# Clamps ahead of sums on GpSimd, a fourth weight chunk finished later and ScalarE's bits a step early, in an FFT-mixing and feed-forward kernel

## The chip, the cores and the metric

The kernel runs on one core of one Trainium2 chip. The metric is the device time of one launch in microseconds (us). The core has a matrix engine (TensorE, PE in the profile), VectorE (DVE), ScalarE (ACT), GpSimd (POOL) and a queue engine that issues transfers (SP). Each has its own instruction stream, and engines wait for each other by semaphores.

## The reference

```python
# x (8, 3008, 256) f32, w_in (256, 2048) f32, w_out (2048, 256) f32
X = np.fft.fft(np.fft.fft(x, axis=1), axis=2).real.astype(np.float32)
t = X.reshape(8 * 3008, 256)
h = t @ w_in
g = h * (1.0 / (1.0 + np.exp(-1.702 * h)))
out = (g @ w_out).astype(np.float32)        # (24064, 256)
```

## The kernel before

Almost all of the time is a loop of 384 steps: TensorE makes two blocks of hidden values (`hidden`, tiles pa and pb), VectorE combines them (`rows`), ScalarE applies the activation (`activate`), and TensorE multiplies by the second weights three steps later (`product`, tile po). This is about the first 82 us, in which weights are prepared while the first transform runs.

Weights arrive in eight 1 MB chunks of 64-bit numbers (in0 to in3, out0 to out3) and are rounded to 32 bits on the chip. For one chunk:

```python
def squares(key, eng): ...        # L368, VectorE or ScalarE: g = hi * hi
def clamp(key, lo=0, n=1024):     # L371, GpSimd: m = min(max(hi, -TOP), TOP)
    nc.gpsimd.tensor_scalar(...)
def low_up(key): ...              # ScalarE: the low bits, first half
def low_down(key): ...            # L381, ScalarE: the low bits, second half -> r
def bounds(key):
    prepare(key); squares(key, nc.scalar); clamp(key); low_up(key); low_down(key)
def high(key, lo=0, n=1024):      # VectorE, needs g and m; a is a single buffer
    dve.scalar_tensor_tensor(m, g, LOW * LOW, m, ...)    # L398
    dve.tensor_scalar(a, bits, ...)                      # L399
    dve.scalar_tensor_tensor(a, bits, 0xC0000000, a, ...)# L400
def finish_in(n, ...):            # L412, GpSimd: wst = a + r, an integer sum
def finish_out(n): ...            # L420, GpSimd: wo = a + r, two sums
def round_chunk(key):
    bounds(key)
    high(key)
    (finish_out if key[0] == "out" else finish_in)(key[1])
# ... cut ...
def fold_w(n, between=()):        # TensorE: 2 x 2 passes of 512 columns, tile psw;
    ...                           # ScalarE copies psw into wcs after each two
def first_row(n):                 # TensorE: one-column products, tile psf -> af2
```

An in-chunk goes on to TensorE (`fold_w`), which multiplies it by a small cosine and sine matrix; only then can steps use it. Steps 0 to 3 of the loop use the folds of in0 and in1, steps 4 to 7 those of in2 and in3, and so on in turn. PSUM tiles of folds, first rows, stage two and hidden values share four banks in turn. The part ahead of the loop, and the loop's schedule:

```python
            for h0 in (0, 512):          # in0 in two halves
                clamp(in0, h0, 512)
                high(in0, h0, 512)
                finish_in(0, h0, 512)
    # ... loads issued, cut ...
    squares(in1, nc.vector); clamp(in1); low_up(in1); low_down(in1); high(in1); finish_in(1)
    fold_w(0)
    prepare(out0); squares(out0, nc.vector); clamp(out0); low_up(out0); low_down(out0)
    high(out0); finish_out(0)
    warm(3)                              # matmuls whose result nobody reads
    rotate(0, 0, 4, nc.scalar.copy)
    stage2(0, 0)                         # second stage of the transform: PE, then VectorE transposes
    prepare(in2); squares(in2, nc.scalar); clamp(in2)
    fold_w(1, ((low_up, in2), (low_down, in2)))
    high(in2); finish_in(2)
    first_row(0)
    # ... cut ...
    for t, key in (2, ("out", 1)), (3, ("in", 3)), (5, ("out", 2)), (6, ("out", 3)):
        at(t, round_chunk, key)
    early[2], early[4] = 2, 3            # fold_w(2) in step 2, fold_w(3) in step 4
    rows_at = {1: 1, 3: 2, 5: 3}         # first_row
    for t in range(n + LAG):             # LAG = 3
        if t < n: hidden(t)
        if t == 0: nyquist(0, 0)         # the broadcast row that rows() needs
        if t in rows_at: first_row(rows_at[t])
        if t >= LAG: product(t - LAG)
        if t in early: fold_w(early[t])
        # activate(t-1), sums, rows(t), combine, then what at() put there
```

## Time and profile before

| | before |
|---|---|
| time, three runs | 1932.56 us (1932.33 to 1935.51) |
| the profiled execution | 1935.1 us, span 1933.3 us |
| PE busy in the first 82 us | 69.22 us |
| PE busy from 82 to 1900 us | 1818.00 us of 1818.00 |
| PE at half clock, up to its last matmul | 17.1 us, in three stretches |

One thing about this table matters for everything below: the execution that was profiled took 1935.1 us, so it is a slow one of its kind by 2.5 us.

In rows in order of time, the columns are: start in us, busy us, engine, line, operation, output<-input, shape, how many instructions were joined, and in brackets the idle time before them with what ended it.

### The profile page before, as it was taken

The numbers are of one execution on the slowest core, as the hardware profiler recorded it, in microseconds if no ns is written. First come the engines' busy times: TensorE is split into PE (matmuls) and PEld (weight loads), VectorE is DVE, ScalarE is ACT, GpSimd is POOL, SyncE is SP. The second block draws the span as 40 slices with busy tenths as digits, with TensorE's granted clock in tenths as the row PEclk, the third lists the DMA queues.
The fourth block names the chain that finished last, engine by engine and source line by source line (L and its number), as shares of the span: only waits on it lengthen the run. The fifth ranks groups of instructions, "written<-read, shape, count | busy, mean of one in ns | idle before, by whom it ended". The sixth has DMA issues, their size and how long they took to land.

```text
span 1933.3 us, 29337 instructions
## 1 busy us (share of the span) xinstructions
PE 1914.2 (99%) x10722; PEld 1677.6 (87%) x10722; DVE 1414.6 (73%) x2937; ACT 670.7 (35%) x923; POOL 764.0 (40%) x1057
## 2 busy tenths in 40 slices
PE   8899999999999999999999999999999999999998
PEld 5698888988889888898889888898888988889887
DVE  6577776877778677876777777777776777777776
ACT  4533333333333333333333333333333333333332
POOL 4275323543246332562235523265323642223222
PEclk9899999999999999999999999999999999999999
DMA  8620450227203362125322162221720223202201
GB/s 289 151 49 10 103 71 12 49 55 113 17 12 59 49 109 17 22 48 102 56 28 48 35 94 47 22 49 43 115 25 13 17 46 58 17 12 27 17 12 23
DMA packets 144912, 103.54 MB, mean 54 GB/s; under 512 B 104770, under 2 KB 127586, under 8 KB 143584
## 3 DMA queue, kind: packets, MB, share of 16 engines
q1 hardware_dynamic: 143424, 100.62, 31.1%
q8 instruction: 85, 1.39, 0.3%
q10 hardware_dynamic: 1344, 1.05, 0.2%
q14 instruction: 59, 0.48, 0.1%
HBM read 58.38 MB, written 48.01 MB: 55 GB/s over the span
## 4 chain that ended last, share of the span: by engine, by line
PE 96%; DVE 1%; DMA 1%; POOL 1%; issue 0%; ACT 0%; SPq 0%; POOLq 0%; DVEq 0%
PE po L542 59%; PE pa L475 17%; PE pb L475 17%; PE ps L213 1%; PE ps L320 1%; DMA raw<-in_moe_w_in_dram 1%; PE psw L439 1%; POOL wst L412 0%; DMA xt<-in_x_dram 0%; DVE m L398 0%; POOL m L371 0%; DVE a L400 0%; PE ps L217 0%; DVE a L399 0%; POOL wo L420 0%
## 5 line engine op out<-in xcount | busy, mean ns | idle before, releaser
L542 PE MATMUL po<-s,wo 128*128 128x256 f32 (+1 forms) x3008 | 758.7, 375 | 0.0
L516 POOL TENSOR_TENSOR s<-h 128x256 f32<-128x256 f32 (+1 forms) x376 | 270.6, 720 | 1086.2 <-ACT h L504 1021.6
L542 PE MATMUL po<-h,wo 128*128 128x256 f32 (+1 forms) x2384 | 689.7, 375 | 0.0
L542 PEld LDWEIGHTS po<-s,wo 128*128 128x128 f32 x3008 | 571.5, 190 | 64.5
L479 ACT COPY v<-pa 128x512 f32<-128x512 f32 (+1 forms) x384 | 222.0, 578 | 1062.4 <-PE pa L475 1062.4
L489 DVE TENSOR_TENSOR h<-v,pb 128x512 f32<-128x512 f32 (+1 forms) x384 | 258.8, 674 | 394.7 <-PE pb L475 390.8
L542 PEld LDWEIGHTS po<-h,wo 128*128 128x128 f32 x2384 | 452.8, 190 | 51.6
L504 ACT ACTIVATE h<-h 128x1024 f32<-128x1024 f32 (+1 forms) x384 | 400.8, 1044 | 17.9 <-DVE h L499 16.3
L475 PE MATMUL pa<-pq,wcs 128*128 128x256 f32 (+1 forms) x1536 | 394.2, 379 | 0.2 <-ACT af L452 0.2
L475 PE MATMUL pb<-pq,wcs 128*128 128x256 f32 (+1 forms) x1536 | 388.4, 375 | 0.0
L492 DVE SCALAR_TENSOR_TENSOR dif<-nb,af,pb 128x256 f32<-128x256 f32 (+1 forms) x768 | 328.1, 468 | 0.0
L475 PEld LDWEIGHTS pa<-pq,wcs 128*128 128x128 f32 x1536 | 286.8, 190 | 47.5 <-issue 10.8
L475 PEld LDWEIGHTS pb<-pq,wcs 128*128 128x128 f32 x1536 | 292.4, 190 | 33.4
L517 POOL TENSOR_TENSOR s<-h 128x256 f32<-128x256 f32 (+1 forms) x376 | 276.5, 735 | 0.0
L499 DVE TENSOR_TENSOR h<-pa,dif 128x512 f32<-128x512 f32 (+1 forms) x448 | 265.4, 604 | 13.2
L520 DVE TENSOR_TENSOR s<-h,s 128x256 f32<-128x256 f32 (+1 forms) x376 | 198.9, 529 | 12.9
L519 DVE TENSOR_TENSOR s<-s,h 128x256 f32<-128x256 f32 (+1 forms) x376 | 180.4, 480 | 4.3 <-POOL s L516 4.3
L199 POOL TENSOR_TENSOR xt<-xt 111x510 f32<-111x510 f32 x56 | 73.4, 1311 | 4.4
L576 DVE TENSOR_TENSOR c<-u,po 128x256 f32<-128x256 f32 (+1 forms) x188 | 69.3, 409 | 1.6
L326 DVE STREAM_TRANSPOSE pq<-ps 128x256 f32<-128x256 f32 x96 | 34.6, 417 | 43.9 <-PE ps L320 43.9
L576 DVE TENSOR_TENSOR u<-u,po 128x256 f32<-128x256 f32 (+1 forms) x141 | 57.6, 409 | 9.5 <-ACT u L547 4.6
L559 DVE STREAM_TRANSPOSE os<-c 128x512 f32<-128x512 f32 x94 | 61.0, 686 | 0.1
(72 smaller groups left out, 509.9 us busy)
## 6 DMA issues: line engine op xcount, KB each, us to landing
out_dram<-os SPq DMA_DIRECT2D x284, 64.0 KB
Td<-xt SPq DMA_DIRECT2D x14, 768.0 KB
t<-Td SPq DMA_DIRECT2D x7, 1536.0 KB
xt<-in_x_dram SPq DMA_DIRECT2D x14, 512.0 KB
xt<-Xr SPq DMA_DIRECT2D x14, 512.0 KB
nb<-pq SPq DMA_DIRECT2D x23, 256.0 KB
out_dram<-os SPq DMA_DIRECT2D x96, 56.0 KB
Xr<-in_x_dram SPq DMA_DIRECT2D x7, 752.0 KB
```

The costliest lines, as they stand in the source:

```text
L475: nc.tensor.matmul(ps[:, i * 256:i * 256 + n], lhsT=wcs[cs][:, f * 128:(f + 1) * 128], rhs=pq[:, cs, ks], start=True, stop=True)
L479: nc.scalar.copy(two(v[:], n), two(pa[:], n))
L489: nc.vector.tensor_tensor(two(h[:], n), two(v[:], n), two(pb[:], n), op=ALU.add)
L492: nc.vector.scalar_tensor_tensor(dif[:, i * 256:i * 256 + n], nb[:, ks], af2[:, f:f + 1], pb[:, i * 256:i * 256 + n], op0=ALU.mult, op1=AL ...
L499: nc.vector.tensor_tensor(free(h[:], 512 + at + m - 1, [256, 2], [RUN, blocks], [-1, m]), *ins, op=ALU.add)
L504: nc.scalar.activation(g, g, ACTF.Gelu_apprx_sigmoid)
L516: eng.tensor_tensor(s1, a21, a22, op=ALU.add)
L517: eng.tensor_tensor(s3, a11, a21, op=ALU.subtract)
L519: eng.tensor_tensor(s2, s1, a11, op=ALU.subtract)
L520: eng.tensor_tensor(s4, a12, s2, op=ALU.subtract)
L542: nc.tensor.matmul(pot[q][:, i, :n], lhsT=lhs, rhs=rhs, start=(p == 0 and i == 0 and f == 0), stop=(p == NP - 1), skip_group_check=True)
L576: nc.vector.tensor_tensor(out_, i0, i1, op=how)
```

## The change

The intent is to take three waits out of the first 82 us. On GpSimd, the clamp of the next chunk goes ahead of the sum of the last, so that VectorE always has a clamped chunk to work on. The high part and sum of in2, the third in-chunk to be folded (fourth to be rounded, after in0, in1 and out0), go into the loop behind VectorE's rows of steps 0 and 1, and the folds of in2 and in3 come one step later. For chunks in the loop, ScalarE's work and the clamp (`bounds`) come one step before VectorE's high part, and the sum one step after.

```diff
-    def round_chunk(key):
-        bounds(key)
-        high(key)
+    def finish(key):
         (finish_out if key[0] == "out" else finish_in)(key[1])
 # ... one memset placed later, warm(7) is warm(6): cut ...
             for h0 in (0, 512):
                 clamp(in0, h0, 512)
+            for h0 in (0, 512):
                 high(in0, h0, 512)
-                finish_in(0, h0, 512)
 # ... loads: cut ...
     prepare(in1)
+    clamp(in1)
     squares(in1, nc.vector)
-    clamp(in1)
+    for h0 in (0, 512):
+        finish_in(0, h0, 512)
     low_up(in1)
     low_down(in1)
     high(in1)
-    finish_in(1)
+    warm(4)
     fold_w(0)
     prepare(out0)
+    clamp(out0)
+    finish_in(1)
     squares(out0, nc.vector)
-    clamp(out0)
+    warm(1)
+    rotate(0, 0, 4, nc.scalar.copy)
+    stage2(0, 0)
     low_up(out0)
     low_down(out0)
-    high(out0)
-    finish_out(0)
-    warm(3)
-    rotate(0, 0, 4, nc.scalar.copy)
-    stage2(0, 0)
     prepare(in2)
     squares(in2, nc.scalar)
     clamp(in2)
     fold_w(1, ((low_up, in2), (low_down, in2)))
-    high(in2)
-    finish_in(2)
+    high(out0)
+    finish_out(0)
     first_row(0)
 # ... cut ...
-    for t, key in (2, ("out", 1)), (3, ("in", 3)), (5, ("out", 2)), (6, ("out", 3)):
-        at(t, round_chunk, key)
-    early[2], early[4] = 2, 3
-    rows_at = {1: 1, 3: 2, 5: 3}
+    for t, key in (1, in2), (2, ("out", 1)), (3, ("in", 3)), (5, ("out", 2)), (6, ("out", 3)):
+        at(t, high, key)
+        if key != in2:
+            at(t - 1, bounds, key)
+        at(t + 1, finish, key)
+    early[3], early[5] = 2, 3
+    rows_at = {1: 1, 4: 2, 6: 3}
```

More of the change, by code (lines that the diff above doesn't have):

```diff
@@ L617 @@
             room[g] = odds[i][:, 4 * k:4 * k + 4, :]
-    nc.vector.memset(wcs[0][:, 0:512], 1.0)
     for i, (lo, e) in enumerate(zip((0, 24, 8, 16), odds)):
         (nc.vector, nc.gpsimd)[i % 2].memset(xt[96:128, lo:lo + 8, 0:H + 1], 0.0)
+        if i == 0:
+            nc.vector.memset(wcs[0][:, 0:512], 1.0)
+    for e in odds:
         nc.gpsimd.memset(e[64:128], 0.0)
@@ L632 @@
     load_in(1, nc.sync)
-    warm(7)
+    warm(6)
     nc.scalar.activation(af2[0:1, 0:1], ones[0:1, 0:1], ACTF.Gelu_apprx_sigmoid)
```

## The prediction

> **What bounds the kernel now.** I read the summary rows first, then PE alone in order of time, then GpSimd (POOL) alone, then the totals of waits of the first 82 us. Lines of different views are parted by "...":
>
> ```profile
> PE 1914.2 (99%) x10722; PEld 1677.6 (87%) x10722; DVE 1414.6 (73%) x2937; ACT 670.7 (35%) x923; POOL 764.0 (40%) x1057
> ...
> 0.00:82.00 82.00, 69.22 (x347) 45.94 (x347) 50.67 (x74) 37.07 (x52) 33.35 (x31) 0.90 0.76 236
> ...
> 82.00:1900.00 1818.00, 1818.00 (x10253) 1608.23 (x10253) 1345.41 (x2825) 626.05 (x862) 723.54 (x1016) 1.00 0.30 46
> ```
>
> Columns of the last two rows: stretch, its length, busy us of PE, PE's weight loads, DVE, ACT and POOL, then the granted clock. From 82 us to 1900 us PE is busy in all of 1818.00 us at clock 1.00. No reordering can help there, and the diff touches nothing there: only the start can move. It holds 82.00 - 69.22 = 12.8 us of idle PE, and work done at clock 0.5. Where:
>
> ```profile
> 31.28 5.47 PE L439 MATMUL psw<-wst,small 128*128 128x512 f32 x6 [3.66 <-POOL wst L412]
> 36.56 2.77 PE L289 MATMUL warm<-wcs 128*128 128x512 f32 x6
> ...
> 51.70 1.05 PE L451 MATMUL psf<-twos,wcs 1*128 1x1 f32 x8 [1.35 <-DVE dif L492]
> 53.00 1.45 PE L475 MATMUL pa<-pq,wcs 128*128 128x256 f32 x4 [0.25 <-ACT af L452]
> ...
> 75.62 6.35 PE L439 MATMUL psw<-wst,small 128*128 128x512 f32 x8 [3.97 <-POOL wst L412]
> ...
> 26.41 0.65 POOL L371 TENSOR_SCALAR m<-raw 128x512 f32<-128x512 f32 x1
> 29.12 2.10 POOL L412 TENSOR_TENSOR wst<-a,r 128x512 uint32<-128x512 uint32 x1 [2.06 <-DVE a L400]
> 31.20 1.09 POOL L371 TENSOR_SCALAR m<-raw 128x1024 f32<-128x1024 f32 x1
> 35.68 3.21 POOL L412 TENSOR_TENSOR wst<-a,r 128x1024 uint32<-128x1024 uint32 x1 [3.40 <-DVE a L400]
> ...
> 73.22 2.35 POOL L412 TENSOR_TENSOR wst<-a,r 128x1024 uint32<-128x1024 uint32 x1 [3.42 <-DVE a L400]
> ...
> POOL wst L412 <- DVE a L400: 14.4, 5, 3.4
> DVE m L398 <- POOL m L371: 12.4, 6, 3.4
> PE psw L439 <- POOL wst L412: 8.6, 3, 4.0
> ```
>
> A weight chunk passes POOL (clamp, L371), DVE (L398 to L400) and POOL again (sum, L412), and PE folds it (psw). POOL's program has each clamp behind the sum of the chunk before, so POOL and DVE wait for each other in turn (14.4 and 12.4 us). PE waits 8.6 us at the end of that. At 51.70 PE waits for DVE for another reason: the third chunk (in2) stands ahead of step 0's rows on DVE, so rows 0 start only at 50.18.
>
> **What the Trainium skill says.** "TensorE: Matmul & The Clock Gate", Part 1: PE's clock is halved after an idle window and released after a busy one; windows are 3413 ns and free-running. The trace agrees. In slices of half a microsecond the clock is 0.5 over about 29.9-36.6, 53.7-57.1 and 74.3-81.0 us; all six edges fall on one grid of 3.41 us. Windows with about 1 to 2 us of (partly one-column) matmuls ended in a halving. So each gap costs twice: a pass of 512 columns takes 0.43 us at full clock (3.45 us per eight) but 5.47/6 = 0.91 at 31.28.
> "SBUF — State Buffer", section "Who interferes with whom": a DVE instruction with two SBUF inputs, or in a 2-port mode, and a GpSimd instruction that reads SBUF exclude each other, whole instruction by whole instruction. The trace agrees for sums of two tensors: the 512-wide sum took 1.26 us alone, but 2.10 when issued at 29.12 during a DVE square (28.89-30.11): 0.99 us of waiting, then 1.11. L398 to L400 are of these kinds too, yet never overlap POOL work here; that they also lock is the page's word.
>
> **The change part by part.** No arithmetic is added; PE gets one more warming matmul (7+3 become 6+4+1). DVE's early memset exchange puts warming about 1 us later; its end stays near 9.8 us, and the first-batch stage (PE dense from 11.3 to 25.5) waits for DVE and DMA, not for warming: 0.
>
> (a) Four warming matmuls ahead of the first fold: 25.5 + 8 x 0.43 = 28.9 us. They bridge the gap that halved the clock, so the last six passes after 31.28 should take 2.6 instead of 5.47.
>
> (b) Clamps ahead of sums. DVE no longer waits for clamps, but now locks POOL out. Serial from 23.11 on: clamp 0.65, high part of half one 1.81 (0.69 + 0.43 + 0.69), clamp of in1 1.10, half two 1.81, two sums of 1.11, square 1.22 = 8.8, so 31.9 us for the second sum (30.7 if the square falls behind it), against 31.22 before: nothing won there. Next: in1's high part 1.23 + 0.69 + 1.23 = 3.15, clamp of out0 1.10, square 1.22, sum 2.22 = 7.7, so 38.4 to 39.6 for in1's sum, against 38.89. PE does the second fold then, not at 40.46: stage two (about 1.2 us) lies before it, in the wait. At full clock it ends at 41.9 to 43.1; but PE idles about 1.5 to 2.5 us before it, and a halved window would make that 43.7 to 44.8. I take 43.7 against 44.16: **0.5 us won**.
>
> (c) Let H be the start of step 0's first matmul (45.38 before, some 44.9 after). DVE does rows 0 and 1 before in2's high part now. Rows 0 wait for the broadcast row (H+3.7) and end at H+5.3 instead of 52.37 = H+7.0. The first-row matmul, whose bank is freed by rows 0's dif (H+4.6), finds it free: the 1.35 us are gone, and with them the halving at 53.7.
>
> (d) in2's fold moves behind step 3 and product 0. Chain: rows 1 end H+7.45, high part 3.15 gives H+10.6, sum 0.1 + 2.35 gives H+13.05. PE arrives at 9.7 + 3.45 = H+13.15. No wait, but a thin fit.
>
> (e) ScalarE's bits and the clamp a step early: high parts find their inputs. ACT reaches v of step 2 at H+10.5 and of step 3 at H+15.4, because the bits (1.15 + 1.15 + 1.06 = 3.3 us) stand ahead; rows 3 end about H+19.7, and PE waits 0.7 us for a bank before the third first-row. in3: high part ends H+23.2, sum H+25.7; PE reaches the last fold at H+29.05, as step 5 and product 2 (5.2 us) now come ahead. So the 3.97 us and the halving after them go.
>
> Sum from H to the end of the last fold. Before: 81.97 - 45.38 = 36.6 us. In it: idle 1.35 + 0.25 + 3.97 = 5.6; slow clock 6.95 - 5.2 = 1.75 (53.00 to 59.95, for 1.73 + 3.45 of work) and 6.18 - 3.45 = 2.7 at 75.62. Together 10.0, of which I expect 0.9 to remain: **9.1 us won**. Equivalently, the last fold ends at H+32.5 = 77.4 with 5.2 us more work already behind it. With (b), 9.6; I keep back 0.6 for hand-offs of 0.1 to 0.15 us (as from L400 to L412) that I didn't count. **1932.56 - 9.0 = 1923.5 us.** Past that point PE has no gap in which the gain could be lost.
>
> **Rivals.**
> R1, the gain goes into a new wait: POOL is in-order, so a clamp ahead of a sum makes it wait for its chunk's landing, and locks stretch (b). For it: in1 lands only near 25.9 us (DMA falls from full to idle there), and 8.8 us of serial locked work leave no slack. Against: later chunks land long before, and everything from H on has DVE rows with one SBUF input. Then H comes 1 to 2 us later than before and the gain is 7: 1926.
> R2, the clock: with the grid at another phase, or with the thin fit in (d) missed, one more halving (1.7 to 2.7 us): 1926. If the fold at 38 to 42 escapes it too, about 1921.5.
> R3, ACT becomes the bound: bits ahead of v copies delay rows 2 and 3. For it: 3.3 us in front of each. Against: DVE would have its high part then anyway. If rows are 2 us later twice, PE idles 3 to 4 us: 1927.
> R4, all hidden anyway: excluded, since the gaps are PE's own and PE is full afterwards. The reverse, over 2%, would need 38.7 us, thrice the start's 12.8 us of idle: excluded too.
>
> **Range and chances.** The three runs before span 3.2 us. R1 to R3 cost 2 to 4 us each, partly exclusive; the lucky clock wins 2. Eight in ten: 1920.5 to 1928.0. All lie within 2% (1894 to 1971), so the chance of that is 0.99; what is left is for a mistake in my reading of the order.
>
> **What would show it.** PE alone: no wait for POOL's sums over 1 us before step 0's first matmul except ahead of the second fold; no 1.35 us at the second first-row; no 3.97 us at the last fold. Clock 1.00 from about 44 us on, with two halvings gone at least. Wait totals: DVE for POOL's clamps from 12.4 us to under 3. POOL: clamps and sums of 1.1 us stretched beyond 2 near 26-37 us if locks are as I say. Dense PE 9 us of work ahead. It is wrong if step 0's first matmul comes at 47 or later (R1), if PE waits for v or DVE between H+10 and H+25 for more than 2 us (R3), or if a clock of 0.5 stands after 50 us (R2).

## The result

The changed kernel took 1923.57 us (median of four runs, 1922.8 to 1925.11); the kernel before took 1933.05 us on the same occasion (four runs, 1932.33 to 1935.51). The ratio is 0.995, with a 95% interval of 0.9932 to 0.9967: a gain of half a per cent, well within 2%. Ratios here are the mean time of one kernel's fast runs over the mean of the other's fast runs of the same rounds, so not quite the ratio of the medians that are quoted. All kernels gave correct results.

The page of the kernel after, and its table of stretches with the columns that the prediction explains:

```profile
PE 1908.0 (99%) x10724; PEld 1674.6 (87%) x10724; DVE 1422.7 (74%) x2937; ACT 670.6 (35%) x923; POOL 765.5 (40%) x1057
...
0.00:82.00 82.00, 75.20 (x408) 53.55 (x409) 63.19 (x86) 47.97 (x65) 39.33 (x34) 1.00 0.88 256
82.00:1900.00 1818.00, 1818.00 (x10251) 1608.39 (x10250) 1350.17 (x2833) 619.70 (x854) 723.05 (x1019) 1.00 0.30 45
```

As predicted, nothing happened behind 82 us. Ahead of it, PE is busy for 6 us more and does 408 instructions instead of 347; the granted clock is 1.00, where it was 0.90. PE alone, after (line numbers are two lower than before):

```profile
29.42 1.13 PE L437 MATMUL psw<-wst,small 128*128 128x512 f32 x2 [0.87 <-POOL wst L412]
31.62 2.84 PE L437 MATMUL psw<-wst,small 128*128 128x512 f32 x6 [1.07 <-POOL wst L412]
37.92 3.70 PE L437 MATMUL psw<-wst,small 128*128 128x512 f32 x8 [1.40 <-POOL wst L412]
47.43 1.05 PE L449 MATMUL psf<-twos,wcs 1*128 1x1 f32 x8
55.99 3.70 PE L437 MATMUL psw<-wst,small 128*128 128x512 f32 x8
71.48 3.60 PE L437 MATMUL psw<-wst,small 128*128 128x512 f32 x8
```

The four folds are whole: six passes take 2.84 us instead of 5.47, the last eight 3.60 instead of 6.35. The second first-row at 47.43 has no wait (it had 1.35), and the last fold has none (it had 3.97). What is left are three waits ahead of the first two folds; the one of 1.07 us ahead of the last six passes is just over the 1 us that the prediction had allowed there. GpSimd and VectorE in that stretch:

```profile
26.02 1.15 POOL L371 TENSOR_SCALAR m<-raw 128x1024 f32<-128x1024 f32 x1 [3.42 <-DMA raw<-in_moe_w_in_dram]
27.12 4.45 POOL L412 TENSOR_TENSOR wst<-a,r 128x512 uint32<-128x512 uint32 x2
33.09 1.47 POOL L371 TENSOR_SCALAR m<-raw 128x1024 f32<-128x1024 f32 x1 [1.52 <-DMA raw<-in_moe_w_out_dram]
34.53 3.34 POOL L412 TENSOR_TENSOR wst<-a,r 128x1024 uint32<-128x1024 uint32 x1
...
26.04 2.20 DVE L368 TENSOR_TENSOR g<-raw 128x1024 f32<-128x1024 f32 x1
28.35 2.10 DVE L398 SCALAR_TENSOR_TENSOR m<-g,m 128x1024 f32<-128x1024 f32 x1
31.60 0.69 DVE L399 TENSOR_SCALAR a<-m 128x1024 uint32<-128x1024 uint32 x1 [1.15 <-POOL wst L412]
```

Clamps now wait for transfers (3.42 and 1.52 us), because they stand first in GpSimd's order. And the two engines get in each other's way as whole instructions: the square took 1.22 us in the kernel before and 2.20 here, L398 1.23 there and 2.10 here, two half sums 4.45 instead of 2 x 1.11. Yet VectorE hardly waits for clamps any more. From the totals of waits of the first 82 us, with columns "us in all, how often, the longest":

```profile
PE psw L437 <- POOL wst L412: 3.3, 3, 1.4
DVE m L398 <- POOL m L371: 0.6, 1, 0.6
```

These were 8.6 and 12.4 us before.

**Three pieces of an execution.** To see where the time went, I cut each traced execution at two marks: the start of GpSimd's first clamp, which is the moment in0 has landed, and H, the start of step 0's first matmul, as in the prediction.

| traced execution | in0 landed | landing to H | H to the end | PE at half clock |
|---|---|---|---|---|
| before | 21.39 | 23.99 | 1887.9 | 17.1 us |
| after | 20.28 | 22.25 | 1878.5 | none |

So 1933.3 - 1921.0 = 12.3 us of span between these two executions are 1.1 of an earlier landing, 1.7 between landing and H, and 9.4 behind H. Is each of these the change's, or one execution's? That is what the experiments had to settle.

### The profile page after: what moved, and what is told of

It is laid out like the page before. It is cut to its first block, busy times and chain, and to the rows that moved or that the text cites.

```text
span 1921.0 us, 29344 instructions
## 1 busy us (share of the span) xinstructions
PE 1908.0 (99%) x10724; PEld 1674.6 (87%) x10724; DVE 1422.7 (74%) x2937; ACT 670.6 (35%) x923; POOL 765.5 (40%) x1057
## 3 DMA queue, kind: packets, MB, share of 16 engines
q8 instruction: 85, 1.39, 0.3%
q10 hardware_dynamic: 1344, 1.05, 0.2%
## 4 chain that ended last, share of the span: by engine, by line
PE 98%; DVE 1%; DMA 1%; POOL 0%; issue 0%; ACT 0%; SPq 0%; DVEq 0%; POOLq 0%
PE po L540 59%; PE pa L473 17%; PE pb L473 17%; PE ps L213 1%; PE ps L320 1%; PE ps L271 1%; PE psw L437 1%; DMA raw<-in_moe_w_out_dram 0%; POOL wst L412 0%; PE ps L217 0%; DMA wo<-in_tab_dram 0%; PE psf L449 0%; DVE wo L245 0%; DVE os L557 0%; DVE a L400 0%
## 5 line engine op out<-in xcount | busy, mean ns | idle before, releaser
L473 PEld LDWEIGHTS pa<-pq,wcs 128*128 128x128 f32 x1536 | 286.8, 190 | 47.9 <-issue 11.2
```

What stands on the lines that cost most here:

```text
L473: nc.tensor.matmul(ps[:, i * 256:i * 256 + n], lhsT=wcs[cs][:, f * 128:(f + 1) * 128], rhs=pq[:, cs, ks], start=True, stop=True)
```

## The experiments

The theory: the change is two gains that add up, a small one in the start and a large one in the loop, where waits were costly because the clock was halved after them. The rivals: the start makes the gain and the loop adds little (or the reverse, with the other part useless); the bridge of warming matmuls is what counts; or single parts of the change, such as ScalarE's early bits, carry the gain.

Two looks set the size of chance: the kernel before once more, and the kernel after once more.

> The kernel before once more, one look. The first trace of it was of a 1935.1 us run, while its median is 1932.6 to 1933.05. Theory (halved clock windows vary with the phase of the grid): the waits of PE for POOL's sums and for DVE come again within 0.3 us each (3.7, 1.35, 4.0 us), the first matmul of step 0 starts within 1 us of 45.4 us, but the number or length of the half-clock stretches may differ from the three of 6.7, 3.3 and 6.6 us, and the span goes with them, 1.5 to 3 us. Rival: the spread has nothing to do with the clock, and all three stretches come again at the same length whatever the time.

> The changed kernel again, on the same chip and in the same rounds as the three others. Theory: 1922.8 to 1925.1 us as before, median near 1923.6; the spread comes from half-clock stretches, none to two (0 to 7 us) in the traced execution, with the same waits of PE within 0.5 us.

The kernel before took 1933.18 us in that look, span 1931.4. The kernel after took 1924.08 us (five runs, 1923.35 to 1925.5) against 1934.24 of the kernel before in the same rounds, ratio 0.9951 (0.9938 to 0.9965); no half clock in its trace either. The pieces of all traced executions, in one table:

| traced execution | start of which | loop of which | in0 landed | landing to H | H to the end | half clock, us |
|---|---|---|---|---|---|---|
| before | before | before | 21.39 | 23.99 | 1887.9 | 17.1 |
| e0_before_again | before | before | 21.28 | 23.97 | 1886.2 | 10.2 |
| e1_start_only | after | before | 20.48 | 22.22 | 1886.4 | 6.8 |
| e1b_start_only_again | after | before | 21.43 | 22.33 | 1887.5 | 10.2 |
| e2_loop_only | before | after | 21.10 | 23.98 | 1878.1 | 3.4 |
| after | after | after | 20.28 | 22.25 | 1878.5 | none |
| e11_after_again | after | after | 20.83 | 22.18 | 1878.6 | none |
| e3_no_bridge | no warm(4) | after | 21.28 | 23.87 | 1878.5 | 6.8 |
| e4_squares_act | squares moved | after | 19.98 | 20.65 | 1878.3 | none |
| e5_bits_same_step | after | bits late | 20.46 | 22.21 | 1880.2 | none |
| e6_in2_before_rows | in2 ahead | in2 ahead | 20.78 | 23.93 | 1878.1 | 3.4 |
| e7_clamp_out0_back | clamp back | after | 21.21 | 21.32 | 1878.3 | none |
| e8_best | rearranged | after | 21.07 | 19.77 | 1878.3 | none |
| e10_last_fold_later | before | fold later | 20.55 | 23.96 | 1883.2 | 10.2 |

Two things can be read at once. The landing of in0 wanders from 19.98 to 21.43 us between executions whatever the kernel is, so the 1.1 us of the 12.3 are no more than chance gives. And the other pieces repeat well: to 0.2 us for one start, and to half a microsecond for the new loop.

The second look at the kernel before also showed what chance does with the clock. Its row of PE alone, then the stretch from 53.7 to 57.1 us in the first look and in the second (length; PE, weight loads, DVE, ACT, POOL; granted clock, DMA share, GB/s):

```profile
51.56 1.05 PE L451 MATMUL psf<-twos,wcs 1*128 1x1 f32 x8 [1.34 <-DVE dif L492]
```

```profile
53.70:57.10 3.40, 3.40 (x8) 2.32 (x8) 1.59 (x4) 0.79 (x2) 0.20 (x1) 0.50 0.00 0
```

```profile
53.70:57.10 3.40, 3.40 (x12) 2.00 (x11) 2.75 (x5) 1.14 (x3) 0.06 (x1) 1.00 0.00 0
```

The wait is the same as in the first look, 1.35 and 1.34 us at nearly the same time, but only the first look had the clock halved after it. The half-clock stretches of a trace begin and end on a grid of 3.41 us, as the prediction says, and its phase differs between executions: in the first look one grid window (50.26 to 53.67 us) held the wait, the first-row and the 0.25 us behind it, in the second an edge at 51.62 us parted the wait from the rest. H to the end differs by 1.7 us for that reason, which is the 1.75 us that the prediction counted for this halving. The first halving, at the first fold, was shorter too (3.4 us instead of 6.8), but landing to H stayed at 23.97 us: with the old start something else sets H, as is shown below.

**The start alone, and the loop alone.**

```diff
 # e1_start_only, against after (e1b_start_only_again is the same kernel): the loop's schedule of before
+    high(in2)
+    finish_in(2)
     first_row(0)
 # ... and round_chunk at t, early = {2: 2, 4: 3}, rows_at = {1: 1, 3: 2, 5: 3}
```

```diff
 # e2_loop_only, against before: the loop's schedule of after, the start of before but for
-    high(in2)
-    finish_in(2)
     first_row(0)
```

> The changed start (clamps ahead of sums, four warming matmuls as a bridge), in2 finished in the start, with the loop of the kernel before (bits, clamp, high part and sum of a chunk in one step, folds in steps 2 and 4). My theory, that most of the gain is in the loop's order: step 0's first matmul near 42.5 us as in the changed kernel, but the wait of about 4 us and the halved clock (2.7 us) at the last fold are back, so 1928 to 1930.5 us. Rival, that the order of POOL in the start is what pays: 1923.5 to 1925.5 us.

> The kernel of e1_start_only once more, one look, since its traced execution (1930.9 us) was the fastest of its five, and had a single half-clock stretch, while its median (1933.4) equals the kernel before. Theory: the slower executions have more half-clock stretches; at a time near 1933.4 I expect two or three of them (10 to 15 us at half clock in all), the new ones at the waits of PE for POOL or DVE that the changed start still has (near 29 to 33, 36.5 to 38, 48 to 49 us), with the same waits of PE as in the first look within 0.3 us each. Rival: one stretch as in the first look, and a wait that has grown by 2 us or more somewhere else.

> The start of the kernel before (sum before the next clamp, three warming matmuls after the fold) without in2's last part, and the changed loop (in2's high part behind rows 0 and 1, bits one step ahead, folds in steps 3 and 5). My theory: step 0's first matmul at 45 to 45.5 us, from there to the end of the last fold 32.5 us as in the changed kernel instead of 36.6, so 1925 to 1927.5 us. Rival (start pays): 1930 to 1932 us.

The loop alone met its expectation: 1925.59 us (1924.69 to 1927.02) against 1933.3, ratio 0.9959 (0.9945 to 0.9973), and H to the end as in the kernel after. The start alone missed in time: 1933.38 us (1930.9 to 1935.05), ratio 0.9996 (0.9984 to 1.0009), no gain resolved where 1928 to 1930.5 us was expected, and the second look gave 1933.05. The traced places were as expected: H at 42.70 us in e1, and the wait (4.05 us) and the slow fold (6.32 us) at the last fold back. Landing to H is shorter by 1.7 us in both looks. What else the traces show, first e1 on VectorE, then e1b on PE:

```profile
45.79 0.69 DVE L399 TENSOR_SCALAR a<-m 128x1024 uint32<-128x1024 uint32 x1 [2.37 <-POOL wo L420]
```

```profile
39.15 3.70 PE L439 MATMUL psw<-wst,small 128*128 128x512 f32 x8 [2.58 <-POOL wst L412]
49.87 1.05 PE L451 MATMUL psf<-twos,wcs 1*128 1x1 f32 x8 [1.14 <-DVE dif L492]
51.17 1.88 PE L475 MATMUL pa<-pq,wcs 128*128 128x256 f32 x4 [0.25 <-ACT af L452]
```

In e1, in2's high part stands ahead of rows 0, as in the kernel before, and waits 2.37 us for GpSimd's sum of out0, which still reads the only buffer `a` (in the kernel before it waited 2.44 us for its clamp instead). Rows 0 come late, and PE waits 1.51 us at the second first-row. In e1b the waits of 1.14 and 0.25 us were followed by a halving from 51.4 us, in which step 2's hidden values took 3.4 us where 1.83 is usual: 1.6 us, as much as the start had won. But the first look of the kernel before had such a halving too, and H to the end is the same with either start (1886.4 and 1887.5 us here, 1886.2 and 1887.9 there). So it is not shown that the changed start loses its gain in the old loop. The interval of e1 reaches from 3.1 us faster to 1.7 us slower than the kernel before, so a gain of 1.7 us is well inside it; the slowest execution of e1 (1935.05 us) is not among those traced, and what it looks like stays open. What the runs show is thus: the loop's share in time (7.7 us), the start's in the traces alone (1.7 us).

e1b missed its expectation in one point: its wait ahead of the second fold was 2.58 us and not 1.39 as in e1, yet the fold behind it was whole (3.70 us).

Why H comes earlier at all is in one row that stands in each trace with the old start. PE alone in e0, with VectorE's transposes, then PE in e2, then both engines in the kernel after:

```profile
44.30 1.02 PE L451 MATMUL psf<-twos,wcs 1*128 1x1 f32 x8 [1.23 <-DVE pq L326]
...
43.05 1.44 DVE L326 STREAM_TRANSPOSE pq<-ps 128x256 f32<-128x256 f32 x4
```

```profile
44.14 1.02 PE L449 MATMUL psf<-twos,wcs 1*128 1x1 f32 x8 [1.21 <-DVE pq L326]
```

```profile
41.55 1.05 PE L449 MATMUL psf<-twos,wcs 1*128 1x1 f32 x8
...
36.56 1.44 DVE L326 STREAM_TRANSPOSE pq<-ps 128x256 f32<-128x256 f32 x4 [0.92 <-PE ps L320]
```

With the old start, step 0 follows a first-row that waits for VectorE's transposes of stage two, which hold the bank and stand behind out0's high part. The wait is 1.23 and 1.21 us where the first fold lost 3.4 us at half clock (e0, e2), and 0.27 and 0.48 us where it lost 6.8 (the first look of before, e10), but H comes 23.96 to 23.99 us after the landing in all four: the transposes set it, and not PE's clock. The new order puts the transposes first, and the row has no such wait. The prediction read the execution with 0.27 us, where this was hard to see.

**The bridge.**

```diff
 # e3_no_bridge, against after
-    warm(4)
     fold_w(0)
```

> The changed kernel without the four warming matmuls ahead of the first fold. My theory: PE is nearly idle from 25 to 29.4 us, a window of the clock grid ends with the clock halved between 28 and 32 us in most executions, the last six passes of the first fold take about 5 us instead of 2.8, step 0's first matmul comes 1 to 3 us later than at 42.5, and the time is 1924.5 to 1927 us. Rival (the wait for POOL's second chunk hides it, as the second fold waits for the sum anyway): 1923 to 1924 us.

It took 1924.12 us (1923.12 to 1925.44), ratio 0.9951 (0.9939 to 0.9964), a little under what was expected and not to be told from the kernel after. Its trace, PE alone:

```profile
29.15 5.62 PE L437 MATMUL psw<-wst,small 128*128 128x512 f32 x8 [3.84 <-POOL wst L412]
```

Without the four matmuls PE waits 3.84 us in one piece, the clock is halved twice (29.1 to 32.5 and 39.4 to 42.8 us), and H comes 1.6 us later after landing. So the bridge does in the trace what it is for, but its worth in time is not resolved; in this traced execution, which was the slowest of the five, it is 1.6 us.

**The locks, and the clamp of out0.**

```diff
 # e4_squares_act, against after
-    squares(in1, nc.vector)
     for h0 in (0, 512):
         finish_in(0, h0, 512)
+    squares(in1, nc.scalar)
 # ...
-    squares(out0, nc.vector)
     warm(1)
     rotate(0, 0, 4, nc.scalar.copy)
     stage2(0, 0)
+    squares(out0, nc.scalar)
```

```diff
 # e7_clamp_out0_back, against after
-    clamp(out0)
     finish_in(1)
+    clamp(out0)
```

> The changed kernel with the squares of in1 and out0 on ScalarE instead of VectorE. Theory (VectorE's two-input work and GpSimd's reads exclude each other): GpSimd's two sums of in0 take 2.3 to 3.3 us together instead of 4.45, in1's sum about 2.3 instead of 3.34, and the second fold starts near 36.7 us instead of 37.9; 1921.5 to 1923.0 us. Rival (no exclusion, the long instructions are only waiting for data): the sums keep 4.4 and 3.3 us and the time stays 1923 to 1924.

> The changed kernel with one clamp, that of out0, put back behind in1's sum on GpSimd. In the changed kernel this clamp waited 1.5 us for its chunk to land and then ran for 1.5 us in front of the sum that PE's second fold needs. Theory: the sum starts at about 33.7 instead of 34.5 us, the second fold at 37.0 to 37.4 instead of 37.9, and the time is 0.5 to 1 us lower, 1922.5 to 1923.3, at the edge of what five rounds resolve; the trace decides. Rival (clamp ahead pays here too, since out0's high part then waits for it): 1924 to 1925.5 us.

Squares on ScalarE: 1921.96 us (1920.68 to 1923.38), ratio 0.994 (0.9927 to 0.9954), as expected. GpSimd's sums in that kernel:

```profile
26.77 3.47 POOL L412 TENSOR_TENSOR wst<-a,r 128x512 uint32<-128x512 uint32 x2
33.59 2.38 POOL L412 TENSOR_TENSOR wst<-a,r 128x1024 uint32<-128x1024 uint32 x1
```

They took 4.45 and 3.34 us with the squares on VectorE, so each square cost its sum about one microsecond, and landing to H falls from 22.2 to 20.65. That the long sums were a lock between the two engines, and not a slow sum, is thus shown by taking the other party away.

The clamp of out0 put back behind in1's sum: 1922.76 us (1922.13 to 1923.75), ratio 0.9943 (0.9931 to 0.9956), as expected. Against the kernel after, which ran in other rounds, that is not resolved in time. In the trace, the sum no longer stands behind a clamp that waits for its transfer; it waits for VectorE, its real supplier:

```profile
34.65 3.23 POOL L412 TENSOR_TENSOR wst<-a,r 128x1024 uint32<-128x1024 uint32 x1 [2.13 <-DVE a L400]
```

Landing to the second fold takes 16.7 us instead of 17.6, and landing to H 21.3 instead of 22.2. This one clamp, then, was not worth placing ahead; the part of the change's rule that it stands for costs 0.9 us in these traces. The clamp of in1, which waited longer (3.42 us) in front of in0's two sums, stayed where it is in every run with the new start, so what its place costs is open.

**The parts of the loop.**

```diff
 # e5_bits_same_step, against after: bounds at t, right ahead of high
-            at(t - 1, bounds, key)
+            extra[t].insert(len(extra[t]) - 1, (bounds, (key,)))
```

```diff
 # e6_in2_before_rows, against after
     finish_out(0)
+    high(in2)
+    finish_in(2)
     first_row(0)
 # ... and (1, in2) taken out of the loop's list
```

```diff
 # e10_last_fold_later, against before
-    early[2], early[4] = 2, 3
-    rows_at = {1: 1, 3: 2, 5: 3}
+    early[2], early[5] = 2, 3
+    rows_at = {1: 1, 3: 2, 6: 3}
```

> The changed kernel with square, clamp and low bits of the last four chunks moved back into the step of their high part (still finished one step later). Theory: the bits a step early are not what pays; VectorE waits 1 to 2 us for squares in steps 2 and 3, but in3's sum had 3.3 us of slack before the last fold, so PE waits less than 1 us more: 1923 to 1925 us. Rival (the bits' early place is essential): in3's sum comes more than 3.3 us later, PE waits and the clock is halved, 1926 to 1930 us.

> The changed kernel with in2's high part and sum put back in the start, ahead of rows 0 on VectorE (in2 is no longer finished behind stage two's turns and the first rows). Theory, from e1_start_only: in2's high part waits for GpSimd's sum of out0 (the buffer a is single), rows 0 come 2 us later, PE waits about 1.5 us at the second first-row matmul, sometimes with a halved clock behind it (1.75 us): 1925 to 1927.5 us. Rival (VectorE has 2.5 us free there, so in2 costs nothing): 1923 to 1924.3.

> The kernel before with one thing changed in PE's order alone: the last fold of a weight chunk (and its first-row matmul) one step later, behind step 5's hidden matmuls and product 2. Theory: these are 5.2 us of work that PE can do while GpSimd finishes in3's sum, 4.0 us late; the wait at the last fold and the halved clock behind it (2.7 us) both go, so 6 to 7 us won, 1926 to 1928 us. Rival (the wait moves on to another place, product 2 or the banks of step 5): less than 3 us won, 1930.5 to 1933.5 us.

Bits in the same step as the high part: 1924.84 us (1924.66 to 1927.17), ratio 0.9955 (0.9942 to 0.9967), against 1924.08 of the kernel after in the same rounds. H to the end is longer by 1.7 us. That is more than the "less than 1 us" that was expected, though the time is in the expected range. VectorE waits 1.55 and 1.71 us for clamps, and PE for VectorE at a bank:

```profile
68.85 1.13 PE L473 MATMUL pb<-pq,wcs 128*128 128x256 f32 x4 [1.24 <-DVE dif L490]
```

The run moves three things together: ScalarE's square and bits, and GpSimd's clamp. In this trace the two waits are for the clamp, which stands behind the sum of the chunk before on GpSimd: in step 3 ScalarE's square had ended at 62.4 us, and the clamp ended at 64.2. So of `bounds` a step early it is the clamp that these waits point to; a run that moves ScalarE's part alone was not made.

in2 ahead of the rows: 1926.34 us (1924.58 to 1928.15), ratio 0.9961 (0.9948 to 0.9973). The time is as expected, about 2.3 us above the kernel after, but its traced execution, the fastest of the five, lost the time elsewhere than I had said: its second fold ran at half clock, so that H came 1.7 us later and the second first-row then found its bank free. The wait that I had expected for in2's high part is there on VectorE, for the single buffer `a`. First PE, then VectorE:

```profile
38.41 5.40 PE L437 MATMUL psw<-wst,small 128*128 128x512 f32 x8 [1.91 <-POOL wst L412]
...
45.73 0.70 DVE L399 TENSOR_SCALAR a<-m 128x1024 uint32<-128x1024 uint32 x1 [2.38 <-POOL wo L420]
```

What its slower executions lose, and where, is not traced and stays open.

The last fold one step later in the old kernel: 1929.45 us (1926.98 to 1931.96), ratio 0.9978 (0.9966 to 0.9991), where 1926 to 1928 was expected: partly missed. The wait of 3.97 us at the last fold and the slow fold after it are gone, worth 3.97 + 2.7 = 6.6 us, but H to the end fell by only 3 to 4.7. In the place of the old wait stands a new one, and the clock was halved at 52.4 us in this look:

```profile
73.61 1.13 PE L475 MATMUL pb<-pq,wcs 128*128 128x256 f32 x4 [1.74 <-DVE dif L492]
```

Against the look of the kernel before that had the same halving (1887.9), H to the end fell by 4.7 us, which is the 6.6 less the new wait of 1.74, to 0.2 us. PE now comes to step 5 at once and finds VectorE's rows behind, because VectorE still does the whole of a chunk's work in one go. The other parts of the new loop (`bounds` a step early, sums a step later, in2 behind the rows) supply what is missing: with them, H to the end is 1878.4 instead of 1883.2.

**A version from what was found.** It puts together e4's square of in1 on ScalarE and e7's clamp, keeps out0's square on VectorE but behind the transposes, and moves in2's square behind the first half of the second fold.

```diff
 # e8_best, against after
-    squares(in1, nc.vector)
     for h0 in (0, 512):
         finish_in(0, h0, 512)
+    squares(in1, nc.scalar)
 # ...
-    clamp(out0)
     finish_in(1)
-    squares(out0, nc.vector)
-    warm(1)
+    clamp(out0)
     rotate(0, 0, 4, nc.scalar.copy)
     stage2(0, 0)
+    squares(out0, nc.vector)
 # ...
-    squares(in2, nc.scalar)
     clamp(in2)
-    fold_w(1, ((low_up, in2), (low_down, in2)))
+    fold_w(1, ((low_up, in2), (lambda key: (squares(key, nc.scalar), low_down(key)), in2)))
```

> A version meant to beat both: the changed kernel with in1's square on ScalarE, out0's square on VectorE behind stage two's turns, out0's clamp behind in1's sum, in2's square on ScalarE between the copies' bits of the second fold, and without the single warming matmul after the first fold. Theory: step 0's first matmul at 39.8 to 40.8 us instead of 42.5, all else as in the changed kernel, 1920.5 to 1922.3 us. Rival (ScalarE's copies or the landing of the first stage's data bind, as ScalarE was 0.9 us late with a copy in e4_squares_act): 1922.3 to 1924.

It took 1920.66 us (1920.33 to 1920.88), ratio 0.9931 (0.9918 to 0.9943), as expected, against 1924.08 of the kernel after in the same rounds, whose five runs (1923.35 to 1925.5) do not overlap. PE alone:

```profile
34.85 0.36 PE L306 MATMUL psr<-t,small 128*128 128x4 f32 x2 [0.86 <-DMA t<-Td]
36.23 3.70 PE L437 MATMUL psw<-wst,small 128*128 128x512 f32 x8
```

The second fold has no wait left. What PE waits for ahead of it now is a transfer, the first batch's stage-one result on its way back (0.86 us); ahead of the first fold's two parts, waits of 0.46 and 1.08 us for GpSimd's sums remain. Landing to H is 19.8 us, 2.4 less than in the kernel after, and the median is 3.4 lower.

## Why the prediction was right

The time, 1923.57 us, is 0.1 us from the predicted 1923.5. The steps behind it were less exact than that, and so close a hit is partly luck: the 9.0 us were taken from 1932.56, the kernel before measured 1933.05 on the same occasion, and the gain was 9.5 us there and 10.2 in the rounds of e11.

**(a) The bridge: right.** Six passes took 2.84 us (2.6 predicted) instead of 5.47, and the clock stayed whole; in e3's trace, without the bridge, it did not.

**(b) Up to H: right for in1's sum, wrong in size for H.** Ends are best counted from the landing (21.39 us in the trace that the prediction read). in0's second sum was to end 10.5 us after it (31.9) and ended 11.3 and 11.2 us after it in the two looks, behind in1's clamp, which waited for its transfer; that it ended at 31.57 by the clock is owed to an earlier landing. in1's sum was to end 17.0 to 18.2 us after the landing (38.4 to 39.6) and ended 17.6 and 17.5 after it. H was predicted at about 44.9, 0.5 us won; it was 42.53 and 43.01. Of these 2.4 to 2.9 us won against 45.38, 0.6 to 1.1 are an earlier landing. Landing to H, for which the prediction amounts to 23.5 us, took 22.2. Two terms of the sum were at fault. I charged a halving after the idle time ahead of the second fold, and took the fold's end at 43.7, 22.3 us after the landing; the idle time was 1.40 us, no halving came in either look, and the fold ended after 21.3: 1.0 us. The rest, about 0.2 us, is the first-row's wait for VectorE's transposes (0.27 us in the trace that I read), which I left standing and the change removes. Behind that is an error of mechanism: I took PE's second fold for what sets H in the kernel before, and it was the transposes.

**(c) to (e) The loop: right, nearly to a tenth.** Rows 0 ended at H+5.30 (H+5.3 predicted); in2's sum at H+13.4 (H+13.05) and its fold, the thin fit of (d), at H+13.46 (H+13.15) after a wait of 0.09 us; in3's sum at H+25.6 (H+25.7); the last fold at H+28.95 (H+29.05), ended at H+32.4 (H+32.5). The third first-row had no wait where 0.7 us was predicted, so 0.35 us of idle time remained behind H, not 0.9. (The prediction's two ways to sum the loop's gain are not quite equal: its second, by the end of the last fold, gives 36.6 + 5.2 - 32.5 = 9.3 us and not 9.1.)

**The size of the loop's gain: too large for what it was subtracted from.** 9.1 us were read from an execution of 1935.1 us, which had a halving at 53.7 us that e0 shows need not come, and subtracted from a median of 1932.56. The mean of the four looks with the old loop is 1887.0 us from H to the end (1887.9, 1886.2, 1886.4, 1887.5), and of the seven with H to the end as in the new loop 1878.4: 8.6 us, and 7.6 between the repeated looks e0 and e11. The start gained 1.7 us in the traces, not 0.5. So the loop's term was too large by 0.5 to 1.5 us, the start's too small by 1.2, and 0.6 us were kept back; the closeness of the sum owes something to these errors, which have opposite signs.

**The rivals.** R1 (a new wait on GpSimd) was partly true: clamps waited 3.42 and 1.52 us for transfers. I had said that later chunks land long before they are needed; out0 landed only at 33.09, and e7's trace shows that it cost 0.9 us. It did not undo the gain, because in1's sum still ended inside the predicted range and the fold behind it ran at the whole clock. R2 (one more halving) came in neither look of the kernel after. It did come in e6, whose start is that of the kernel after up to the second fold: there PE waited 1.91 us ahead of that fold, and the fold took 5.40 us; in the two looks of the kernel after it waited 1.40 and 1.37 us. The length of the wait alone does not decide: in e1b, with the same start, it was 2.58 us, and that fold was whole, since an edge of the grid parted the wait into 1.19 and 1.40 us. I cut all fourteen traces along their grids (phase from their half-clock edges) between about 23 and 82 us and added up, in each window that ran at whole clock, PE's idle time and its one-column matmuls. The 14 windows with 1.91 us or more (1.91 to 3.41) all ended in a halving, and none of those with less did (the highest is 1.84). With idle time alone there is no such line: 1.39 us ended in a halving in e1b, 1.67 did not in e1. This was found afterwards, in these traces alone. In e6 all 1.91 us fell into one window; the two looks of the kernel after have at most 1.32 us in any. But its two waits at the first fold (0.87 and 1.07 us, in e11 1.30 and 1.07) lie close enough together for one window at another phase, so a halving remains a risk of this start. R3 (ScalarE as the bound) did not come: PE has no wait above 0.25 us behind H. e5 shows that `bounds` a step early is what keeps it so, with waits that are for GpSimd's clamp and not for ScalarE.

**What carries the explanation of the clock and the locks.** "TensorE: Matmul & The Clock Gate", Part 1, describes the gate as free-running and so variable from run to run, and the two looks of the kernel before agree: equal waits of 1.35 and 1.34 us, one halving. "SBUF — State Buffer", section "Who interferes with whom", says that VectorE's two-input operations and 2-port modes exclude GpSimd's reads for whole instructions. The prediction had to leave it at the page's word for L398 to L400. The trace of after agrees now: L398 took 2.10 us during a sum, against 1.23 in the kernel before, and L399 took 1.46 instead of 0.69 where, at 57.12 us, it fell on a clamp. "PSUM — Partial Sum Buffer", section "Engine vs sequencer instructions", calls the queues of VectorE, ScalarE and GpSimd strictly first in, first out; e1 agrees, where rows 0, whose inputs were ready at about 44.8 us (an estimate: H + 2.1, when they start in the kernel after), stood behind a high part that waited 2.37 us until 45.79.

## What to carry to other kernels

A wait of the busiest engine is worth more than its length when its clock is gated: 3.97 us of waiting and the slow fold behind it cost 6.6, and in the traces a few matmuls without use, placed in another wait, held the clock. But to take away such a wait is not to gain its cost: in e10 a new wait of 1.74 us took back about a quarter of it. On an engine that works in program order, an early place helps only an instruction whose data are there: the clamps ahead of sums fed VectorE, but the one whose transfer was late held up the sum behind it. Where single parts are worth one or two microseconds and times scatter by three, cut the traces at marks that every execution has (here a landing, a first matmul and the end), and take the size of a gain from more than one execution of the kernel before.

## What the Trainium skill lacked or had wrong

- "SBUF — State Buffer", "Who interferes with whom", says that the first to issue holds the shared ports, but not who gets them next when both engines have more work queued. Here they alternated: the square (2.20 us, 1.22 in the kernel before) was followed by the first half sum, this by L398 (2.10 us, 1.23 before), and this by the second half sum; the two sums took 4.45 us instead of 2.2.
- "TensorE: Matmul & The Clock Gate", Part 1, "HAM oscillation — how this bites in real kernels", gives as the abstract rule no idle gaps of PE above about 3.4 us. These runs show that to be too lax: the clock was halved after 1.35 and 0.25 us of idle time about 1.05 us of one-column matmuls in the first look of the kernel before, after 1.14 and 0.25 us in e1b, and after 1.91 us in e6. The one-column matmuls seem to count as idle (R2 above).
- The same Part gives no measure for a partly busy window that I found. In these traces a window of 3.41 us with 1.91 us or more of idle time and one-column matmuls ended in a halving, and one with 1.84 or less did not; a wait of 2.58 us that an edge of the grid parted (e1b) did not either.
- I found on no page how far the landing of a given transfer may wander between executions of one program: in0 landed between 19.98 and 21.43 us over fourteen looks, more than most parts of this change are worth.
